# Expert weights, activations and hidden values as float16 pairs in place of float32r pairs, with scales measured on the chip

## The chip, the cores and the metric

One NeuronCore of a Trainium2 chip runs the whole program. The metric is the device time of one execution in microseconds (us), as a median over runs. TensorE is the matmul engine, VectorE (DVE in the profile), ScalarE (ACT) and GpSimd (POOL) do the elementwise work, SyncE (SP) issues the DMAs. Matmul results land in PSUM, eight banks of 128 x 512 float32; everything else lives in SBUF.

## The reference

```python
# attention: q, k, v are (2, 8, 1152, 64); q is averaged over pairs of rows
q_pool = q.reshape(B, H, S // 2, 2, D).mean(axis=3)
scores = np.matmul(q_pool, k.transpose(0, 1, 3, 2)) / np.sqrt(D)
attn = softmax(scores)                       # with 1e-9 added to the sum
x = matmul(attn, v)  -> (1152, 512)
# experts: E = 4, w1 (4, 512, 1024), w2 (4, 1024, 512)
p = domain_probs / (domain_probs.sum(-1, keepdims=True) + 1e-09)
for e in range(E):
    h = np.maximum(x @ w1[e], 0.0)
    out += p[:, e:e + 1] * (h @ w2[e])
# last layers: w1, w2 (512, 1024), w3 (1024, 1024), w_out (1024, 512)
a = x @ w1;  b = x @ w2
return ((a * b) @ w3) @ w_out
```

All inputs are float32 but those of the last layers, which the kernel reads as 64-bit words and converts on the chip.

## The kernel before

The program has three stages, one after the other on TensorE.

The **attention** runs over eight pairs of heads. An agenda holds closures with times in units of one block of scores (`at(t, f)`); sorted by time, it gives the program order, which each engine then follows. Per pair, `plan_v` measures the range of v: VectorE takes the maximum of each partition (line 409), TensorE transposes the two columns of maxima (413), VectorE reduces them to one number per head and makes a power of two of it in a chain of small operations (418 to 424), a tiny matmul with `ones2` spreads it to all partitions (427), and VectorE copies it (431). v is then held as a float16 high part (ScalarE, 441) and low part (VectorE, 445). The attention's output comes out multiplied back to its own scale into `X`.

The **experts** are cut into 16 groups `g` of 256 hidden columns, `PER` = 4 groups to an expert. Every product is taken from high and low parts, in three passes (`PASSES`: high x high, high x low, low x high). The parts are float32r, a 32-bit form in which the matmul reads float32 data:

```python
nc.scalar.copy(out=dst[:, 0, :], in_=src)
(eng or nc.gpsimd).tensor_tensor(out=dst[:, 1, :], in0=src, in1=f32(dst[:, 0, :]), op=ALU.subtract)
```

`prep_w(g, m)` loads w1 (m = 0) or w2 (m = 1) of a group (512 KB, line 567) into one of two `raw` buffers and splits it: ScalarE the high part (559), GpSimd the low part (560), VectorE for the first three. `rows_tile` transposes 128 rows of x and splits them into `xA` or `xB` (670, 674). `up_tiles` is the first layer: for each half group, a tile of 512 columns (part A, rows 0 to 511 of x) and two of 320 (part B), 12 matmuls each (596); ScalarE takes the result out through Relu as the high part of `h` (602), VectorE makes the low part (606). `down_tiles` is the second layer: nine tiles of 128 rows, 6 matmuls of 512 columns each (636); VectorE multiplies a tile by the token's share of the expert and adds it to `x2A` or `x2B` (648, 650).

`TASKS` sets the order: part A of group 0, part B of group 0, then whole groups 1 to 15. Group 0 begins inside the attention's agenda, at `UA`; in the loop, task n does the first layer of its group, then two calls of `prep_w`, then the second layer of task n - 1. Results rotate through eight banks (`bank`). The weights that are ahead of their use wait in four `spl` buffers.

Beside the loop, `tick` converts weights of the last layers from 64-bit words to float32: a load (700), one pass of ScalarE (705), five operations on VectorE (710 to 720, "a join"), one on GpSimd (723). There is one tick per task from n = 3 and two from n = 9.

The **last layers** multiply w3 by w_out first (1003), then do the gated product (1034) and the output (1051), all float32r, as before and after the change.

Of the kernel before, what the change touches and what calls it, by code (L numbers as in the profile page):

```python
# [47 lines left out]
SW = 130  # L48
W0 = 124
WD = 4  # L50
WS = 6
# [17 lines left out]
AX = mybir.AxisListType  # L69
PSUM = bass.MemoryType.PSUM  # L70


# [7 lines left out]
def tile_kernel(ctx: ExitStack, tc: tile.TileContext, q, k, v, dp, w1, w2, mw1, mw2, mw3, mwo, out):  # L80
# [18 lines left out]
    EPS = 1e-9  # L99

    f32 = lambda ap: ap.bitcast(F32)
    mm = nc.tensor.matmul
# [299 lines left out]
    def plan_v(i, t, te):  # L402


        st = {}

        def rows():
            m = st["m"] = tiny.tile([P, 2], F32, tag="vm", name=f"vm{i}")
            nc.vector.tensor_reduce(out=m, in_=rv[i], axis=AX.X, op=ALU.max, apply_absolute_value=True)  # L409

        def turn():
            st["p"] = work(1, f"vt{i}")
            nc.tensor.transpose(st["p"][0:2, 0, :P], st["m"], ident)
# [12 lines left out]
        def spread():  # L426
            mm(st["p"][:, 0, P : P + 2], ones2, st["d"], start=True, stop=True)

        def keep():
            vs[i] = tiny.tile([P, 2], F32, tag="vs", bufs=3, name=f"vs{i}")  # L430
            nc.vector.tensor_copy(vs[i], st["p"][:, 0, P : P + 2])
# [129 lines left out]

    def prep_w(g, m, eng=None):

        e, o = divmod(g, PER)
        t = raw.tile([P, 2 * DM], F32, tag="raw", name=f"rw{g}_{m}")
        src = (w1[e, :, o * GRP : (o + 1) * GRP], w2[e, o * GRP : (o + 1) * GRP, :])[m]
        nc.sync.dma_start(
            out=t.rearrange("p (c f) -> p c f", f=src.shape[1]), in_=src.rearrange("(c p) f -> p c f", p=P)
        )

        def rest():
            w = (w1s, w2s)[m][g] = spl.tile([P, 2, 2 * DM], F32R, tag="spl", name=f"w{m}_{g}")
            split(t, w, eng)

        return rest

    def up_tiles(n, space, h_tiles):
# [3 lines left out]
        for fc in range(2):  # L581
            for lo, hi in cuts(part):
# [18 lines left out]
                def to_hi(fc=fc, lo=lo, hi=hi, st=st):  # L601
                    nc.scalar.activation(out=hid[n][0][:, fc, lo:hi], in_=st["p"], func=AF.Relu)  # L602

                def to_lo(fc=fc, lo=lo, hi=hi, st=st):
                    hh, hl = hid[n]
                    nc.vector.scalar_tensor_tensor(  # L606
                        out=hl[:, fc, lo:hi], in0=st["p"], scalar=0.0, in1=f32(hh[:, fc, lo:hi]),
                        op0=ALU.max, op1=ALU.subtract,
                    )
# [13 lines left out]
    def down_tiles(n, space):  # L623
        part, g = TASKS[n]
        out_ = []
        for t in blocks(part):
# [14 lines left out]
            def add(t=t, st=st):  # L641
                x = "A" if t < NB else "B"
                if x not in x2:
                    x2[x] = xpool.tile([P, NB + 1, DM], F32, tag="x", name=f"x2{x}")
                acc, e = x2_of(t), g // PER
                share = pr[:, t, e : e + 1]
                if g == 0:
# [8 lines left out]

    def rows_tile(src, t, space, name):

# [4 lines left out]
        def pe():  # L663
            p = st["p"] = space(name)
            for d in range(KD):
                nc.tensor.transpose(p[:, d * P : (d + 1) * P], src(t)[:, d * P : (d + 1) * P], ident)

        def to_hi():
            p4 = st["p"].rearrange("p (d t) -> p d t", d=KD)
            nc.scalar.copy(out=xt[x][0][:, :, sl], in_=p4)  # L670

        def to_lo():
            p4 = st["p"].rearrange("p (d t) -> p d t", d=KD)
            nc.vector.tensor_tensor(  # L674
                out=xt[x][1][:, :, sl], in0=p4, in1=f32(xt[x][0][:, :, sl]), op=ALU.subtract
            )

        return pe, to_hi, to_lo

    def new_xt(x, pool, name):  # L680
        n = NTA if x == "A" else NTB
        xt[x] = [pool.tile([P, KD, n], F32R, tag=f"x{x}{m}", name=f"{name}{x}{m}") for m in range(2)]

# [44 lines left out]
    with tc.manual_schedule():  # L728
# [86 lines left out]
        def h_small(n):  # L815
            return [ha_p.tile([P, 2, NTA], F32R, tag=f"ha{m}", name=f"ha{n}_{m}") for m in range(2)]

        def plan_w(g, m, t):
            st = {}

            def load():
                st["rest"] = prep_w(g, m, nc.vector)

            at(t, load)
            at(t + WS, lambda: st["rest"]())

        for n, (g, m) in enumerate(((0, 0), (0, 1), (1, 0))):
            plan_w(g, m, W0 + WD * n)
        at(SW, experts)
        at(SW, new_xt, "A", xa_p, "x")  # L830
        at(SW, lambda: nc.sync.dma_start(out=XT[0:64], in_=X[0][64:128, NB, :]))
        t = SW + XA
        for n in range(NB):
            pe, to_hi, to_lo = rows_tile(x_src, n, one_bank, f"xt{n}")
            at(t + XS * n, pe)
# [4 lines left out]
        def rows_b():  # L840
            kstack.close()
            xb_p.append(ctx.enter_context(tc.tile_pool(name="xb_p", bufs=1, side="left")))
            new_xt("B", xb_p[0], "x")

# [15 lines left out]
        for _, _, f, args in sorted(agenda, key=lambda x: x[:2]):  # L860
# [4 lines left out]
        (r4, h4, l4), (r5, h5, l5), (r6, h6, l6), (r7, h7, l7), (r8, h8, l8) = (  # L865
            rows_tile(x_src, t, s_bank if t < 6 else one_bank, f"xt{t}") for t in range(NB, 9)
        )
# [17 lines left out]
    def h_large(n):  # L885
        return [h_p.tile([P, 2, NT], F32R, tag="h", name=f"h{n}_{m}") for m in range(2)]

    wo_s = [wo_p.tile([P, 2, 2, DM], F32R, name=f"wo{n}") for n in range(4)]

    with tc.manual_schedule():  # L890
# [52 lines left out]

        last_task = len(TASKS) - 1
        for n in range(1, last_task + 1):
            ups = up_tiles(n, bank, h_large)
            for num, steps in enumerate(ups):
                run(steps)
                if num == 2 and n >= 3:
                    tick(NF + 12)  # L950
            g = TASKS[n][1]
            if g + 2 < NG:
                prep_w(g + 2, 0)()
            if g + 1 < NG:
                prep_w(g + 1, 1)()
            if n > 1:
                for num, steps in enumerate(down_tiles(n - 1, bank)):
                    run(steps)
                    if num == 4 and n >= 9:
                        tick(NF + 12)  # L960
# [135 lines left out]
```

## Time and profile before

| | |
|---|---|
| median of 3 runs | 884.58 us (884.54 to 886.27) |
| profiled execution, its own time | 885.5 us |
| its span, first to last instruction | 883.7 us |
| mean granted TensorE clock | 0.992 |
| TensorE matmuls busy | 851.2 us, 96% |
| VectorE, ScalarE, GpSimd busy | 557.1, 358.7, 378.9 us |
| second layer of the experts, matmuls | 840 of 395 ns, 24 of 412 ns |
| first layer, 512 and 320 columns | 384 of 391 ns, 768 of 309 ns |

Matmuls overlap in the engine, so the length of one is more than the distance to the next: the busy time of a line says little, the distance between starts says what a matmul costs. Idle time of an engine matters only where another waits for it; the chain of waits tells that, followed back from the last instruction. PEclk in the windows is the granted share of TensorE's full clock.

### The profile page before, as it was taken

To read this page: it belongs to the slowest core of one execution; us is meant where nothing else is said; L and a number is where in the kernel's file an instruction comes from. 1 tells how busy PE (TensorE), PEld (TensorE's weight loads), DVE (VectorE), ACT (ScalarE), POOL (GpSimd) and SP (SyncE) were. 2 spreads that over 40 slices of the span, in tenths; PEclk is the share of its full clock that TensorE was granted. 3 is DMA by queue.
4 is the path that set the end of the run, shared out by engine and by line. 5 is a ranking of instruction groups with operands and counts; after the bars stand their busy time and mean duration, and the time that the engine had idled before them with its cause. 6 is when DMAs were issued, how large, how long until landed. Compare 5 with 4: busy or idle time off the path is not lost.

```text
span 883.7 us, 15735 instructions
## 1 busy us (share of the span) xinstructions
PE 851.2 (96%) x6356; PEld 737.9 (83%) x6356; DVE 557.1 (63%) x892; ACT 358.7 (41%) x632; POOL 378.9 (43%) x297
## 2 busy tenths in 40 slices
PE   7699999999999999999999999999999999998998
PEld 5588888888878888888888888888888889988887
DVE  6888988898785343455456665656567874996000
ACT  2577878787873312222222232222204333333211
POOL 4487888778751312223223343232210244666200
PEclk9799999999999999999999999999999999999999
DMA  8565756683540220211223223212210320330011
GB/s 189 152 145 147 174 140 149 142 175 91 128 121 3 96 71 24 72 39 36 70 72 96 77 90 96 96 46 75 72 48 1 95 93 28 96 96 24 12 48 47
DMA packets 59831, 76.72 MB, mean 87 GB/s; under 512 B 23480, under 2 KB 41264, under 8 KB 59760
## 3 DMA queue, kind: packets, MB, share of 16 engines
q1 hardware_dynamic: 59760, 75.73, 31.8%
q8 instruction: 50, 0.82, 0.4%
q14 instruction: 21, 0.17, 0.1%
HBM read 51.92 MB, written 2.36 MB: 61 GB/s over the span
## 4 chain that ended last, share of the span: by engine, by line
PE 70%; DVE 21%; issue 4%; DMA 2%; ACT 1%; SPq 1%; POOL 0%; DVEq 0%; ACTq 0%; POOLq 0%
PE up L596 23%; PE dn L636 22%; DVE mx L340 6%; PE o L1051 6%; PE wf L1003 5%; PE gt L1034 5%; PE s L465 3%; DVE vt L445 3%; PE mp L337 2%; DVE cv_a L716 2%; PE av L511 1%; DVE cv_a L710 1%; DVE cv_a L713 1%; DVE vm L409 1%; DVE pl L486 1%
## 5 line engine op out<-in xcount | busy, mean ns | idle before, releaser
L636 PE MATMUL dn<-w,h 128*128 128x512 f32 x840 | 199.6, 395 | 0.0
L636 PEld LDWEIGHTS dn<-w,h 128*128 128x128 f32 x840 | 156.5, 187 | 36.6
L486 POOL TENSOR_TENSOR pl<-p,ph 128x576 f16<-128x576 f32 x124 | 167.0, 1361 | 42.5 <-ACT ph L481 34.3
L560 POOL TENSOR_TENSOR w<-rw,w 128x1024 fp32r<-128x1024 f32 x29 | 69.6, 2401 | 196.0 <-ACT w L559 184.7
L606 DVE SCALAR_TENSOR_TENSOR h<-up,h 128x320 fp32r<-128x320 f32 (+1 forms) x94 | 51.6, 554 | 106.7 <-ACT h L602 106.7
L596 PE MATMUL up<-xB,w 128*128 128x320 f32 x768 | 118.3, 309 | 0.0
L596 PEld LDWEIGHTS up<-xB,w 128*128 128x128 f32 x768 | 115.0, 188 | 2.8 <-issue 0.3
L340 DVE TENSOR_REDUCE mx<-mp 128x1 f32<-128x768 f32 (+1 forms) x144 | 101.8, 750 | 21.6 <-PE mp L337 21.3
L465 PE MATMUL s<-Q,K 128*128 128x288 f32 x576 | 111.8, 318 | 0.6 <-DMA Q<-ml 0.5
L474 ACT ACTIVATE p<-s 128x576 f32<-128x576 f32 x144 | 93.5, 649 | 35.9 <-PE s L465 28.4
L602 ACT ACTIVATE h<-up 128x320 fp32r<-128x320 f32 (+1 forms) x94 | 46.0, 489 | 131.8 <-PE up L596 131.0
L596 PE MATMUL up<-xA,w 128*128 128x512 f32 x384 | 94.1, 391 | 0.4 <-DVE xA L674 0.4
L559 ACT CAST w<-rw 128x1024 fp32r<-128x1024 f32 x32 | 33.4, 1047 | 141.9 <-PE dn L636 83.8
L465 PEld LDWEIGHTS s<-Q,K 128*128 128x128 f32 x576 | 84.8, 194 | 1.4 <-issue 0.6
L511 PE MATMUL av<-vt,ph 128*128 128x65 f16 x720 | 82.3, 193 | 1.0 <-DVE XT L526 0.9
L596 PEld LDWEIGHTS up<-xA,w 128*128 128x128 f32 x384 | 71.0, 188 | 14.5 <-DVE xA L674 0.7
L511 PE MATMUL av<-vt,pl 128*128 128x65 f16 x720 | 82.4, 195 | 0.6 <-DVE pl L486 0.6
L481 ACT ACTIVATE ph<-s 128x576 f16<-128x576 f32 x128 | 82.7, 646 | 0.0
L509 PE MATMUL av<-vt,ph 128*128 128x64 f16 x720 | 81.6, 193 | 0.0
L511 PEld LDWEIGHTS <-ph 128*128 128x128 f16 x720 | 66.8, 99 | 7.6 <-DVE XT L526 2.2
L650 DVE SCALAR_TENSOR_TENSOR x2B<-dn,pr,x2B 128x512 f32<-128x512 f32 x75 | 54.6, 749 | 26.0 <-PE dn L636 25.6
L509 PEld LDWEIGHTS <-ph 128*128 128x128 f16 x720 | 66.7, 97 | 5.1 <-issue 2.3
(137 smaller groups left out, 1282.7 us busy)
## 6 DMA issues: line engine op xcount, KB each, us to landing
rw<-in_moe_w SPq DMA_DIRECT2D x64, 512.0 KB
K<-kab SPq DMA_DIRECT2D x32, 288.0 KB
rk<-in_k SPq DMA_DIRECT2D x16, 288.0 KB
rv<-in_v SPq DMA_DIRECT2D x8, 576.0 KB
Q<-qh SPq DMA_DIRECT2D x32, 144.0 KB
K<-kl SPq DMA_DIRECT2D x16, 288.0 KB
rq<-in_q SPq DMA_DIRECT2D x8, 512.0 KB
rw<-in_moe_w_out SPq DMA_DIRECT2D x8, 512.0 KB
```

The costliest lines, as they stand in the source:

```text
L340: nc.vector.tensor_reduce(out=mx[i, s][:, j, g : g + 1], in_=st.pop((j, g))[:, :, :PC], axis=AX.XY, op=ALU.max)
L465: mm(ps[:, n, :HALF], a[s][:, cs], b[s][:, n * HALF : (n + 1) * HALF], start=first, stop=not first,)
L474: nc.scalar.activation(out=two(p32), in_=st["s"][:, :, :HALF], func=AF.Exp, scale=SCORE)
L481: nc.scalar.activation(out=two(o), in_=st["s"][:, :, :HALF], func=AF.Exp, scale=SCORE)
L486: eng.tensor_tensor(out=plt[i, s][:, c, :], in0=st["p"], in1=pht[i, s][:, c, :], op=ALU.subtract)
L509: mm(t[:, j, 0:D], p, vt[s][:, c, 0:D], start=False, stop=False)
L511: mm(t[:, j, :], p, vt[s][:, c, D:], start=(c == 0 and n == 0), stop=(c == NC - 1 and n == 2))
L560: (eng or nc.gpsimd).tensor_tensor(out=dst[:, 1, :], in0=src, in1=f32(dst[:, 0, :]), op=ALU.subtract)
L596: mm(p, w[:, a, c, fc * P : (fc + 1) * P], x[b][:, c, lo - o : hi - o], start=(c == 0 and a == b), stop=(c == KD - 1 and a == 1),)
L636: mm(p, hid[n][a][:, fc, t * P : (t + 1) * P], w[:, b, fc, :], start=(fc == 0 and a == b), stop=(fc == 1 and a == 1),)
L650: nc.vector.scalar_tensor_tensor(out=acc, in0=st["p"], scalar=share, in1=acc, op0=ALU.mult, op1=ALU.add)
L1051: mm(p, gt[c][:, a, t * P : (t + 1) * P], wf[c][:, b, lo:hi], start=(m == 0), stop=(m == 23))
```

## The change

Both layers' operands (weights, x, h) become float16 pairs. float16 has a short range, so each operand is scaled by a power of two taken from a range measured on the chip, and the scales are taken out again in the share by which a tile is added.

- The range of x is bounded by that of v: per batch, the smallest of the v scales (`cxp`, `cx`), one small operation per pair and, after the last pair of a batch, `at_rows`, four small operations that also fold the reciprocal and `HDOWN` into the shares `prx`.
- The range of a group's weights is measured as that of v is: `prep_w` now returns six steps for both weights of a group: `load` (two DMAs), `rows` (two maxima on VectorE), `turn` (a transpose on TensorE and a chain of six small operations on VectorE), `spread` (a tiny matmul with `ones2`, a copy, and the group's shares), and `cut(0)`, `cut(1)` (ScalarE the high part, VectorE the low part). GpSimd has no splits of expert weights any more. One `spl` buffer now holds both weights of a group.
- Group 0's steps stand in the agenda from `W0`, group 1's from `W1`, at the offsets `WT`. In the loop, `weights(n)` runs after each tile and takes the next step when `WN` tiles have gone by since the last one and the group is near enough (three tasks ahead for the first four steps, two for the cuts).
- `to_hi` of the first layer becomes two passes of ScalarE: Relu with 1 / `HDOWN` in place in PSUM, then a copy to float16.

```diff
+    def at_rows(b):
+        nc.vector.tensor_reduce(out=cx[:, b : b + 1], in_=cxp[:, b], axis=AX.X, op=ALU.min)
+        nc.vector.reciprocal(out=cxi[:, b : b + 1], in_=cx[:, b : b + 1])
+        for r, ts in ((slice(0, P), slice(NB * b, NB * b + NB)), (slice(64 * b, 64 * b + 64), slice(8, 9))):
+            nc.vector.tensor_scalar(
+                out=prx[r, ts], in0=pr[r, ts], scalar1=cxi[r, b : b + 1], scalar2=HDOWN, op0=ALU.mult, op1=ALU.mult
+            )
...
+    def prep_w(g, space, eng=None):
...
+        def rows():
+            st["m"] = wtiny.tile([P, 2], F32, tag="wm", name=f"wm{g}")
+            for m in range(2):
+                nc.vector.tensor_reduce(
+                    out=st["m"][:, m : m + 1], in_=raws[m], axis=AX.X, op=ALU.max, apply_absolute_value=True
+                )
+
+        def turn():
+            p = space(f"wr{g}")
+            nc.tensor.transpose(p[0:2, :P], st["m"], ident)
...
+            nc.vector.tensor_reduce(out=a[:, 0:1], in_=p[0:2, :P], axis=AX.X, op=ALU.max)
...
+        def spread():
+            p = space(f"ws{g}")
+            mm(p[:, :4], ones2, st["d"], start=True, stop=True)
+            wab[g] = wtiny.tile([P, 4], F32, tag="wab", name=f"wab{g}")
+            nc.vector.tensor_copy(wab[g], p[:, :4])
...
+        def cut(m):
+            if m == 0:
+                w = spl.tile([P, 2, 2, 2 * DM], F16, tag="spl", name=f"w{g}")
+                w1s[g], w2s[g] = w[:, 0], w[:, 1]
...
+            nc.scalar.activation(out=w[:, 0], in_=raws[m], func=AF.Copy, scale=c)
+            (eng or nc.vector).scalar_tensor_tensor(
+                out=w[:, 1], in0=raws[m], scalar=c, in1=w[:, 0], op0=ALU.mult, op1=ALU.subtract
+            )
...
-                    nc.scalar.activation(out=hid[n][0][:, fc, lo:hi], in_=st["p"], func=AF.Relu)
+                    nc.scalar.activation(out=st["p"], in_=st["p"], func=AF.Relu, scale=1 / HDOWN)
+                    nc.scalar.copy(out=hid[n][0][:, fc, lo:hi], in_=st["p"])
...
-        return [h_p.tile([P, 2, NT], F32R, tag="h", name=f"h{n}_{m}") for m in range(2)]
+        return [h_p.tile([P, 2, NT], F16, tag="h", name=f"h{n}_{m}") for m in range(2)]
...
+        coming = [(1, 1, later[0])]
+        for g in range(2, NG):
+            coming += [(g if k < 4 else g + 1, w, f) for k, (f, w) in enumerate(zip(prep_w(g, bank), WN))]
+        wait = [0]
+
+        def weights(n):
+            wait[0] += 1
+            while coming and wait[0] >= coming[0][1] and coming[0][0] <= n + 2:
+                wait[0] = 0
+                coming.pop(0)[2]()
...
                 run(steps)
+                weights(n)
                 if num == 2 and n >= 3:
                     tick(NF + 12)
-            g = TASKS[n][1]
-            if g + 2 < NG:
-                prep_w(g + 2, 0)()
-            if g + 1 < NG:
-                prep_w(g + 1, 1)()
```

Line numbers in the orders below are those of each program itself. VectorE in the late loop, around the first layer of task 11 (h is a low part, cv_a to r a join). Before:

```order
L606 SCALAR_TENSOR_TENSOR h_1_7045<-up_0_0_7046,h_0_7044 128x512
L606 SCALAR_TENSOR_TENSOR h_1_7045<-up_0_512_7061,h_0_7044 128x320
L606 SCALAR_TENSOR_TENSOR h_1_7045<-up_0_832_7076,h_0_7044 128x320
L710 TENSOR_SCALAR cv_a<-cv_a 128x512
L713 TENSOR_SCALAR cv_a<-cv_a 128x512
L716 SCALAR_TENSOR_TENSOR cv_a<-rw_6902,cv_a 128x512
L719 TENSOR_SCALAR r_0_7093<-cv_a 128x512
L720 SCALAR_TENSOR_TENSOR r_0_7093<-rw_6902,r_0_7093 128x512
L606 SCALAR_TENSOR_TENSOR h_1_7045<-up_1_0_7104,h_0_7044 128x512
L606 SCALAR_TENSOR_TENSOR h_1_7045<-up_1_512_7119,h_0_7044 128x320
```

The same stretch now, from the maxima (wm) of group 12 to the start of its chain (wa):

```order
L611 TENSOR_REDUCE wm_7372<-rw_0_7326 128x1
L611 TENSOR_REDUCE wm_7372<-rw_1_7328 128x1
L689 TENSOR_TENSOR h_1_7355<-up_0_512_7375,h_0_7354 128x320
L689 TENSOR_TENSOR h_1_7355<-up_0_832_7391,h_0_7354 128x320
L812 TENSOR_SCALAR cv_a<-cv_a 128x512
L815 TENSOR_SCALAR cv_a<-cv_a 128x512
L818 SCALAR_TENSOR_TENSOR cv_a<-rw_7194,cv_a 128x512
L821 TENSOR_SCALAR r_0_7409<-cv_a 128x512
L822 SCALAR_TENSOR_TENSOR r_0_7409<-rw_7194,r_0_7409 128x512
L689 TENSOR_TENSOR h_1_7355<-up_1_0_7420,h_0_7354 128x512
L689 TENSOR_TENSOR h_1_7355<-up_1_0_7420,h_0_7354 128x512
L689 TENSOR_TENSOR h_1_7355<-up_1_512_7436,h_0_7354 128x320
L620 TENSOR_REDUCE wa_7454<-wr_7452 2x1
```

The two maxima stand ahead of the join, and the chain, which the tiny matmul needs, behind it.

TensorE in the same task, at the step from second-layer tile 0 to tile 1 (dn is the tile, h and w its operands). Before:

```order
L636 MATMUL dn_0_7159<-w_9_6756,h_1_6845 128x512
L636 MATMUL dn_0_7159<-w_9_6756,h_0_6844 128x512 x2
L636 MATMUL dn_0_7159<-w_9_6756,h_1_6845 128x512
L636 MATMUL dn_1_7167<-w_9_6756,h_0_6844 128x512 x2
L636 MATMUL dn_1_7167<-w_9_6756,h_1_6845 128x512
```

And now, with the tiny matmul (ws) of group 12:

```order
L718 MATMUL dn_0_7478<-w_6889,h_0_7130 128x512
L718 LDWEIGHTS h_1_7131
L718 MATMUL dn_0_7478<-w_6889,h_1_7131 128x512
L637 MATMUL ws_7486<-wd_7455,ones_74 128x4
L718 LDWEIGHTS h_0_7130
L718 MATMUL dn_1_7492<-w_6889,h_0_7130 128x512
```

The tiny matmul stands between the two tiles, and tile 1 cannot start before it.

## Rows read from the trace of the kernel before

**Rows 1.** The chain in order of time: start us, us, what.

```profile
319.68 12.60 PE dn L636 x54
332.28 12.49 PE up L596 x72
...
645.89 18.20 PE dn L636 x78
```

**Rows 2.** Windows: us; busy PE, PEld, DVE, ACT, POOL; PEclk; DMA.

```profile
332.28:357.37 25.09, 25.09 (x127) 21.66 (x127) 10.11 (x15) 5.49 (x9) 4.81 (x2) 1.00 0.06 22
507.92:533.01 25.09, 25.09 (x128) 21.65 (x127) 16.18 (x26) 7.23 (x12) 10.04 (x6) 1.00 0.27 90
```

**Rows 3.** Timeline of one period: start us, us, engine line op out<-in xcount.

```profile
532.86 2.88 PE L596 MATMUL up<-xA,w 128*128 128x512 f32 x12
...
535.58 3.68 PE L596 MATMUL up<-xB,w 128*128 128x320 f32 x24
...
540.17 0.42 DVE L710 TENSOR_SCALAR cv_a<-cv_a 128x512 f32<-128x512 f32 x1
...
542.28 0.69 DVE L720 SCALAR_TENSOR_TENSOR r<-rw,r 128x512 f32<-128x512 uint32 x1
```

**Rows 4.** Timeline of TensorE, float16 matmuls of the start and of the attention.

```profile
13.06 0.45 PE L752 MATMUL warm<-idle 128*128 128x128 f16 x5
...
14.39 1.68 PE L752 MATMUL warm<-idle 128*128 128x128 f16 x27
...
269.80 0.20 PE L511 MATMUL av<-vt,ph 128*128 128x65 f16 x1
...
270.49 0.19 PE L509 MATMUL av<-vt,ph 128*128 128x64 f16 x1
```

**Rows 5.** Timeline, the range of v in the last pair, 216 to 219 us.

```profile
216.48 0.27 PE L413 MATMUL vt<-ident,vm 128*2 128x128 f32 x1 [0.29 <-DVE vm L409]
...
216.59 0.19 PE L511 MATMUL av<-vt,ph 128*128 128x65 f16 x1
...
216.79 0.28 DVE L418 TENSOR_REDUCE va<-vt 2x1 f32<-2x128 f32 x1
...
217.10 0.14 DVE L419 TENSOR_SCALAR va<-va 2x1 int32<-2x1 int32 x1
...
217.64 0.22 DVE L424 TENSOR_SCALAR vd<-ident,va 2x2 fp32r<-2x2 f32 x1
...
217.92 0.27 PE L427 MATMUL vt<-vd,ones 2*128 2x2 f32 x1
...
218.12 0.20 PE L511 MATMUL av<-vt,pl 128*128 128x65 f16 x1
```

**Rows 6.** Lines 409, 445 (duration ns min/median/max); page groups 602, 606, 650.

```profile
L409 DVE TENSOR_REDUCE vm<-rv x8: 1341/1344/1354, 17.2 to 215.0; 128x2 f32<-128x1152 f32 x8
...
L445 DVE SCALAR_TENSOR_TENSOR vt<-rv,vs,vt x16: 814/1802/2252, 27.7 to 261.6; 128x576 f16<-128x576 f32 x16
...
L606 DVE SCALAR_TENSOR_TENSOR h<-up,h 128x320 fp32r<-128x320 f32 (+1 forms) x94 | 51.6, 554 | 106.7 <-ACT h L602 106.7
...
L602 ACT ACTIVATE h<-up 128x320 fp32r<-128x320 f32 (+1 forms) x94 | 46.0, 489 | 131.8 <-PE up L596 131.0
...
L650 DVE SCALAR_TENSOR_TENSOR x2B<-dn,pr,x2B 128x512 f32<-128x512 f32 x75 | 54.6, 749 | 26.0 <-PE dn L636 25.6
```

**Rows 7.** Timeline, load of expert weights, 393 to 401 us.

```profile
393.87 0.94 SPq L567 DMA_DIRECT2D rw<-in_moe_w  x2
...
399.28 1.05 ACT L559 CAST w<-rw 128x1024 fp32r<-128x1024 f32 x1 [3.84 <-DMA rw<-in_moe_w]
```

**Rows 8.** Waits of TensorE: us in total, times, longest.

```profile
PE mp L337 <- DVE vs L431: 1.7, 6, 0.3
```

**Rows 9.** Timeline of VectorE where the experts begin, 242 to 250 us.

```profile
242.98 1.22 DVE L560 TENSOR_TENSOR w<-rw,w 128x1024 fp32r<-128x1024 f32 x1 [1.20 <-ACT w L559]
...
248.62 1.27 DVE L674 TENSOR_TENSOR xA<-xt,xA 128x512 fp32r<-128x512 f32 x2
```

More of the change, by code (lines that the diff above doesn't have):

```diff
@@ L48 @@
 SW = 130
-W0 = 124
-WD = 4
+W0 = 123.5
+W1 = 134
+WT = ((0, 4.6, 6.9, 8.2, 8.4, 10), (0, 7.0, 10.0, 11.5, 13.0))
+WN = (1, 4, 4, 2, 1, 1)
 WS = 6
@@ L116, in tile_kernel @@
     XT = const.tile([P, DM], F32, name="XT")
+    ones2 = const.tile([2, P], F32R, name="ones2")
+    cxp = const.tile([P, B, 2], F32, name="cxp")
+    cx = const.tile([P, B], F32, name="cx")
+    cxi = const.tile([P, B], F32, name="cxi")
+    prx = const.tile([P, 9, E], F32, name="prx")
+    wtiny = ctx.enter_context(tc.tile_pool(name="wtiny", bufs=4, side="left"))
     xstack = ExitStack()
@@ L430, in keep @@
             vs[i] = tiny.tile([P, 2], F32, tag="vs", bufs=3, name=f"vs{i}")
-            nc.vector.tensor_copy(vs[i], st["p"][:, 0, P : P + 2])
+            p = st["p"][:, 0, P : P + 2]
+            nc.vector.tensor_copy(vs[i], p)
+            b, n = divmod(i, NPAIR // B)
+            if n == 0:
+                nc.vector.tensor_copy(cxp[:, b], p)
+            else:
+                nc.vector.tensor_tensor(out=cxp[:, b], in0=p, in1=cxp[:, b], op=ALU.min)
+            if n == NPAIR // B - 1:
+                at_rows(b)
         at(t, rows)
@@ L655, in down_tiles, with rows_tile @@
         return out_
-    def rows_tile(src, t, space, name):
+    def rows_tile(src, t, space, name, scaled=False):
         x, o = ("A", 0) if t < NB else ("B", NB)
@@ L666, in pe, with pieces, new_xt @@
                 nc.tensor.transpose(p[:, d * P : (d + 1) * P], src(t)[:, d * P : (d + 1) * P], ident)
+        def pieces():
+            for b in range(B):
+                if t < 2 * NB and b == t // NB:
+                    yield slice(0, P), sl, cx[:, b : b + 1]
+                if t == 2 * NB:
+                    n = sl.start + 64 * b
+                    yield slice(64 * b, 64 * b + 64), slice(n, n + 64), cx[:, b : b + 1]
         def to_hi():
             p4 = st["p"].rearrange("p (d t) -> p d t", d=KD)
-            nc.scalar.copy(out=xt[x][0][:, :, sl], in_=p4)
+            if not scaled:
+                nc.scalar.copy(out=xt[x][0][:, :, sl], in_=p4)
+                return
+            for a, to, c in pieces():
+                nc.scalar.activation(out=xt[x][0][:, :, to], in_=p4[:, :, a], func=AF.Copy, scale=c)
         def to_lo():
             p4 = st["p"].rearrange("p (d t) -> p d t", d=KD)
-            nc.vector.tensor_tensor(
-                out=xt[x][1][:, :, sl], in0=p4, in1=f32(xt[x][0][:, :, sl]), op=ALU.subtract
-            )
+            if not scaled:
+                nc.vector.tensor_tensor(
+                    out=xt[x][1][:, :, sl], in0=p4, in1=f32(xt[x][0][:, :, sl]), op=ALU.subtract
+                )
+                return
+            for a, to, c in pieces():
+                nc.vector.scalar_tensor_tensor(
+                    out=xt[x][1][:, :, to], in0=p4[:, :, a], scalar=c, in1=xt[x][0][:, :, to],
+                    op0=ALU.mult, op1=ALU.subtract,
+                )
         return pe, to_hi, to_lo
-    def new_xt(x, pool, name):
+    def new_xt(x, pool, name, kind=F32R):
         n = NTA if x == "A" else NTB
-        xt[x] = [pool.tile([P, KD, n], F32R, tag=f"x{x}{m}", name=f"{name}{x}{m}") for m in range(2)]
+        xt[x] = [pool.tile([P, KD, n], kind, tag=f"x{x}{m}", name=f"{name}{x}{m}") for m in range(2)]
     def x_src(t):
@@ L815, in h_small, with plan_w @@
         def h_small(n):
[L816 to L828, printed above, removed]
+            return [ha_p.tile([P, 2, NTA], F16, tag=f"ha{m}", name=f"ha{n}_{m}") for m in range(2)]
+        later = []
+        def plan_w(g, t, space):
+            steps = prep_w(g, space, nc.vector)
+            for f, d in zip(steps, WT[g]):
+                at(t + d, f)
+            if g == 1:
+                later.append(steps[5])
+        plan_w(0, W0, one_bank)
+        plan_w(1, W1, one_bank)
         at(SW, experts)
-        at(SW, new_xt, "A", xa_p, "x")
+        at(SW, new_xt, "A", xa_p, "x", F16)
         at(SW, lambda: nc.sync.dma_start(out=XT[0:64], in_=X[0][64:128, NB, :]))
@@ L865, in tile_kernel @@
         (r4, h4, l4), (r5, h5, l5), (r6, h6, l6), (r7, h7, l7), (r8, h8, l8) = (
-            rows_tile(x_src, t, s_bank if t < 6 else one_bank, f"xt{t}") for t in range(NB, 9)
+            rows_tile(x_src, t, s_bank if t < 6 else one_bank, f"xt{t}", True) for t in range(NB, 9)
         )
@@ L958, in tile_kernel @@
                     run(steps)
+                    weights(n)
                     if num == 4 and n >= 9:
```

58 lines of the change are left out of this document (40 added, 18 removed).

## The prediction, before the changed kernel was run

> **What bounds the kernel now.** I read the chain of waits in order of time first, then the windows and the timeline of the expert stage. Busy TensorE alone would not tell the limit; the chain does: to 664 us it is one unbroken series of expert matmuls, second-layer and first-layer pieces in turn, 27 of them from 320 us on, of which one pair and the last (two tasks' tiles on end) are shown: 12.60 and 12.49 us [rows 1]. A group of 256 expert columns thus costs 25.09 us, and nothing else is ever waited for. The windows, each one such period long, say how much room the other engines have in it: VectorE is busy 10.1 us early in the stage and 16.2 us where the conversions of the last layers ("joins") run beside it [rows 2]. So in this stage a cheaper matmul shortens the time one for one, until VectorE, or a wait for it, takes over.
>
> **The matmuls.** Their number stays. Starts are 12.60 / 54 = 233.3 ns apart in the second layer [rows 1]. In the first, a tile of 512 columns takes 535.58 - 532.86 = 2.72 us for 12 [rows 3], 226.7 ns each, and what is left of 12.49 us for the 48 of 320 columns, (12.49 - 24 x 0.2267) / 48 = 146.9 ns. [...] No float16 matmul of this size is in the trace. [...] I take 3 ns over the columns: 216.3 and 136.3. Saved: 864 x 17.0 = 14.7 us (second layer), 384 x 10.4 = 4.0 us and 768 x 10.6 = 8.1 us (first layer), together **-26.8 us**; the bounds, 4.4 and 2.6 ns, give -24.0 and -27.6.
>
> [...]
>
> **Added on TensorE.** Each of the 16 groups gets one transpose and one tiny matmul that measure its weights' range. The kernel already does this pair for v: after the transpose the next matmul starts 0.11 us later, after the tiny one 0.20 us later [rows 5]. 16 x 0.31 = **+5.0 us**. The bounds are 0 (hidden behind a long matmul) and 8, half as much again, since behind a 512-column matmul nothing like it is in the trace.
>
> **Added on VectorE in the stage.** Per group: two maxima over 128x1024, by the v maximum (1344 ns for 1152 elements [rows 6]) in proportion 1.2 us each, 2.4; the chain of small operations after the transpose, from 216.79 to 217.64 + 0.22 [rows 5] and one more of 0.22, 1.3; a copy and the new shares, 0.35 by the small ones in the same rows; two low parts of 128x1024. The low part of v is the same operation on 576 elements, 814 ns at its shortest and 2252 at its longest [rows 6]; 448 more elements at the maximum's rate of 1.17 ns make 1.34 at best, 2.7 for two. Together 6.7 us on top of 10.1 to 16.2: 16.8 to 22.9 us in a period of 25.09 - 1.68 + 0.31 = 23.7 us. It fits, in the last third barely. GpSimd loses 29 splits, which nobody waited for, so that gains nothing. ScalarE's second pass over each first-layer tile, 0.49 us [rows 6], six times a period, is covered: what it makes is read only a whole first layer later; without that cover it would cost its own length per tile. Loading a group's two weights together moves no more bytes; the queue issues them once both low parts of the group before are done.
>
> **New waits.** Before, TensorE never waited for a range. Now it stops, in program order, at the transpose until both maxima are done, and at the tiny matmul until the chain is; everything behind it on TensorE waits too. The built program puts four tiles between load and maxima, four to the transpose, two to the tiny matmul. Two tiles are 2.6 us of second layer, or 2.9 of both. In that time VectorE must take out the tile before (0.75 us [rows 6], or for a first-layer tile two passes of ScalarE and its own, 0.49 + 0.49 + 0.55) and run the chain, 1.3: 2.05 or 2.8 us. Any backlog is then a wait. A join is a backlog of 542.28 + 0.69 - 540.17 = 2.8 us [rows 3], and it stands between maxima and transpose in groups 5, 11, 12 and 15; I give these 1.5 us each. Five more have their maxima, or what follows them, among second-layer tiles (7, 8, 9, 10, 14), where four tiles are 5.2 us and the weights land 5.4 us after the issue [rows 7]: 0.4 us each. **+8 us**, between 0 and 2.1 us (the join less the slack left) in each of 15 groups, 32.
>
> **In the attention.** After each v scale VectorE does one small operation more (0.14 us [rows 5]), twice a set of four (0.7). Matmuls do wait for that scale, six times [rows 8]. 8 x 0.14 + 1.4 = 2.5 us; I put two thirds on the path, **+1.7**, bounds 0 and 2.5.
>
> **Where the experts begin.** Ahead of the last xA split (end 249.9 us) VectorE now does two maxima, a chain, a copy with shares and one low part where it did one split of 1.22: 2.4 + 1.3 + 0.35 + 1.34 - 1.22 = 4.2 us more, against 1.20 us of idle time there [rows 9]. TensorE's first expert tile needs that split. A third such split, which stood between the two hidden tiles of that layer, moves away, so it may come out less. **+3 us**, bounds 0 and 6.
>
> What follows the experts is not touched: 0. **Sum**: -26.8 + 5.0 + 8 + 1.7 + 3 = -9.1 us, from the profiled execution's 885.5 us 876.4. That execution is 0.9 above the median of the runs, 884.58, so for the median I expect **875.5 us**.
>
> **Rivals.**
> *Nothing waits.* Maxima and chains find room, the start is absorbed. For: VectorE had 9 to 15 us free per period [rows 2]. Against: two tiles are only just as long as the chain. 884.6 - 26.8 + 5.0 + 1.7 + 1 = 865.5 us.
> *TensorE waits for VectorE at every tiny matmul* (slower). VectorE comes to its last third with 22.9 us of work in 23.7, stays late, and each group pays the 2.1 us above: -26.8 + 9.7 + 32 = +15, 899.5 us. It decides from (26.8 - 9.7) / 15 = 1.1 us per group. For: low parts as long as the longest of v, 2252 against 814 ns [rows 6], would take the rest of the room. Against: only the last third is so full, and with eight banks of matmul results VectorE may be late without stopping TensorE elsewhere.
> [...]
> [...]
>
> **How the numbers follow.** Some waits, the forecast: 0.50. Nothing waits: 0.25. Every group waits: 0.21. No faster stream: 0.03. Float16 pays more: 0.01. About 0.2% (1.8 us) is what a measurement of this kernel can tell from no change. The forecast's own range, 865 to 888, comes of -26.8 by 2.5 either way, waits from 2 to 17 and the two starts from 1 to 7; of its half some 0.05 lie within 0.2% of 884.6 and 0.02 are slower. Of the rival with waits in every group, those of 1.0 to 1.2 us fall within 0.2%: 0.04. So faster 0.43 + 0.25 = 0.68, same 0.05 + 0.04 = 0.09, slower 0.23. The range for 8 in 10 leaves out the worse half of the slow rivals and a little below: 864 to 890.
>
> **What would show it.** Second-layer tiles of 1.30 us and first-layer ones of 2.60 and 1.64: the stream is as I say; at 1.40 it isn't. A period of 23.7 us in the early groups and more in the late ones, with TensorE's idle time released by VectorE at the two new matmuls: the waits; a chain that stays on TensorE: the first rival. VectorE busy some 22 us per period in the last third: its load is as reckoned. The last xA split some 3 us later than at 249.9 us: the start. I would be wrong with a wait that I did not name, as for the first use of a group's weights, or with low parts of over 2 us.

## The result: 876.8 us, 0.94% faster

The changed kernel takes **876.77 us** (median of 4 runs, 875.1 to 877.26) against 884.56 for the kernel before (4 runs, 883.93 to 886.27): a ratio of 0.9906, 95% interval 0.9887 to 0.9925. The profiled execution took 875.1 us, its span is 873.3 (before: 885.5 and 883.7).

The chain of waits in order of time (start us, us, what), beside [rows 1]:

```profile
336.04 11.70 PE up L678 x72
347.74 0.11 PE wr L617
347.85 2.59 PE dn L718 x12
350.44 0.20 PE ws L637
350.64 9.17 PE dn L718 x42
```

The first layer's 72 matmuls went from 12.49 to 11.70 us. The second layer's 54 take 2.59 + 9.17 = 11.76 instead of 12.60, and the two new matmuls of a group's range (wr, ws) now stand in the chain with 0.11 and 0.20 us.

The same in the timeline of TensorE, beside [rows 3]:

```profile
335.88 2.75 PE L678 MATMUL up<-xA,w 128*128 128x512 f16 x12
338.47 3.42 PE L678 MATMUL up<-xB,w 128*128 128x320 f16 x24
341.73 2.75 PE L678 MATMUL up<-xA,w 128*128 128x512 f16 x12
```

338.47 - 335.88 = 2.59 us for 12 of 512 columns, 216 ns each (before: 226.7); 341.73 - 338.47 = 3.26 for 24 of 320 columns, 136 ns (146.9).

Windows, one period each (us; busy PE, PEld, DVE, ACT, POOL; PEclk; DMA), beside [rows 2]:

```profile
335.88:359.64 23.76, 23.76 (x129) 12.51 (x128) 15.67 (x28) 8.49 (x15) 0.00 (x0) 1.00 0.31 89
407.31:432.28 24.97, 24.13 (x132) 12.56 (x129) 20.07 (x38) 8.62 (x16) 3.13 (x2) 1.00 0.18 63
503.59:529.88 26.29, 23.88 (x129) 12.44 (x128) 22.35 (x41) 9.56 (x17) 4.76 (x4) 1.00 0.42 121
601.62:624.98 23.36, 23.36 (x128) 12.32 (x126) 14.71 (x26) 6.98 (x14) 2.54 (x2) 1.00 0.15 46
```

Most periods are 23.8 us against 25.09. Two are much longer (the second and the third row, in which the ranges of groups 8 and 12 are measured: 24.97 and 26.29 us), and the one in which no range is measured (last row) takes 23.36. VectorE's busy time rose from 10.1 to 15.7 us early and from 16.2 to some 22 us late.

Where the trace after stands against the one before: the first expert matmul comes at 256.60 instead of 249.14 us (+7.5), the first layer of group 2 at 312.11 instead of 307.02 (+5.1), the last second-layer block at 636.68 instead of 645.73 (-9.0). So up to that block the expert stage gained 16.5 us, and 7.5 had been lost ahead of it. Before, and after, a tile of attention scores (s) and the first expert matmul:

```profile
226.51 0.77 PE L465 MATMUL s<-Q,K 128*128 128x288 f32 x4
...
249.14 0.40 PE L596 MATMUL up<-xA,w 128*128 128x512 f32 x1
```

```profile
231.04 0.77 PE L494 MATMUL s<-Q,K 128*128 128x288 f32 x4
...
256.60 0.39 PE L678 MATMUL up<-xA,w 128*128 128x512 f16 x1
```

More than half of that loss has its place in these rows, VectorE and GpSimd near the end of the attention:

```profile
218.80 4.48 POOL L515 TENSOR_TENSOR pl<-p,ph 128x576 f16<-128x576 f32 x3 [0.30 <-ACT ph L510]
...
220.67 0.17 DVE L462 RECIPROCAL cxi<-cx 128x1 f32<-128x1 f32 x1
220.87 2.44 DVE L464 TENSOR_SCALAR prx<-pr,cxi 128x16 f32<-128x16 f32 x2
...
256.15 1.40 DVE L775 SCALAR_TENSOR_TENSOR xA<-xt,cx,xA 128x512 f16<-128x512 f32 x2
```

The two operations on the shares (prx), of 16 and 4 elements a partition, hold VectorE for 2.44 us beside a series of GpSimd; the same happens at 100.07 us for the first batch. Against the trace before, the score tiles ahead of the first set start 0.9 us earlier and those behind it 1.2 later; at the second set it goes from 1.1 to 4.5 us later. The last xA split ends at 257.55 us (before: 249.89).

### The profile page after: what moved, and what is told of

Same layout as the page of the kernel before. It is cut to its first block, busy times and chain, and to the rows that moved or that the text cites. A ratio compares the mean times of both kernels' runs of the same rounds, so it can differ in the third digit from the quotient of the medians.

```text
span 873.3 us, 16029 instructions
## 1 busy us (share of the span) xinstructions
PE 833.9 (95%) x6388; PEld 597.2 (68%) x6388; DVE 643.4 (74%) x1098; ACT 406.3 (47%) x729; POOL 307.0 (35%) x268
## 4 chain that ended last, share of the span: by engine, by line
PE 64%; DVE 26%; DMA 4%; issue 3%; ACT 1%; SPq 1%; POOL 0%; DVEq 0%; ACTq 0%; POOLq 0%
PE up L678 19%; PE dn L718 18%; PE o L1163 6%; DVE mx L352 5%; PE wf L1115 5%; PE gt L1146 5%; PE s L494 4%; PE mp L349 3%; DVE cv_a L818 2%; DVE vt L474 2%; PE av L540 2%; DVE cv_a L812 2%; DVE cv_a L815 2%; DMA rw<-in_moe_w 1%; DVE w L653 1%
## 5 line engine op out<-in xcount | busy, mean ns | idle before, releaser
L718 PE MATMUL dn<-w,h 128*128 128x512 f16 x840 | 186.4, 379 | 0.0
L678 PEld LDWEIGHTS <-w 128*128 128x128 f16 x1152 | 111.7, 98 | 76.0 <-issue 1.6
L718 PEld LDWEIGHTS <-h 128*128 128x128 f16 x840 | 81.6, 98 | 93.2
L684 ACT ACTIVATE up<-up 128x320 f32<-128x320 f32 (+1 forms) x96 | 45.7, 476 | 171.8 <-PE up L678 171.8
L678 PE MATMUL up<-xB,w 128*128 128x320 f16 x768 | 110.5, 299 | 0.6 <-DVE xB L775 0.5
L689 DVE TENSOR_TENSOR h<-up,h 128x320 f16<-128x320 f32 (+1 forms) x94 | 50.8, 551 | 55.8 <-ACT h L685 55.5
L678 PE MATMUL up<-xA,w 128*128 128x512 f16 x384 | 89.1, 379 | 0.6 <-DVE xA L775 0.6
L825 POOL TENSOR_TENSOR cv_x<-cv_x,cv_a 128x512 f32<-128x512 f32 x24 | 30.8, 1284 | 154.3 <-DVE cv_x L822 154.3
L540 PEld LDWEIGHTS <-pl 128*128 128x128 f16 x720 | 67.0, 98 | 3.9 <-issue 1.1
L349 PE MATMUL mp<-kab,QZ 128*128 128x384 f32 x216 | 58.3, 377 | 7.4 <-DVE mx L352 4.0
```

Source lines behind the costliest of these rows:

```text
L349: mm(ps[:, n, :PC], QZ[:, o : o + P], KAB[i][:, sl], start=True, stop=True)
L540: mm(t[:, j, :], p, vt[s][:, c, D:], start=(c == 0 and n == 0), stop=(c == NC - 1 and n == 2))
L678: mm(p, w[:, a, c, fc * P : (fc + 1) * P], x[b][:, c, lo - o : hi - o], start=(c == 0 and a == b), stop=(c == KD - 1 and a == 1),)
L718: mm(p, hid[n][a][:, fc, t * P : (t + 1) * P], w[:, b, fc, :], start=(fc == 0 and a == b), stop=(fc == 1 and a == 1),)
L825: nc.gpsimd.tensor_tensor(out=x, in0=x, in1=a.bitcast(F32), op=ALU.add)
```

## The experiments

All times are medians against the kernel before, run on the same chip in turn with it; its own medians in these series lie between 884.42 and 884.96 us, so times of two series can be set beside each other to about half a us. A start time in a single trace is looser: the change and four of the runs below, which are alike up to the experts, reach one and the same early score tile at 58.6 to 60.5 us (59.32 in the change, 60.29 before). From that early tile on, distances are steadier: to the score tile shown above it is 166.2 us before and 171.7 in the change, to the first expert matmul 188.9 and 197.3.

Theory after the result: TensorE's gain in the stage is as predicted; what is given back is (a) the two sets on the shares, (b) the ranges' own 0.41 us a group, (c) waits, above all in groups 8 and 12, (d) VectorE's new work where the experts begin. The main rival: VectorE as a whole is the limit, so that whatever is removed at one place comes back at another.

### The shares on GpSimd

```diff
-            nc.vector.tensor_scalar(
+            nc.gpsimd.tensor_scalar(
                 out=prx[r, ts], in0=pr[r, ts], scalar1=cxi[r, b : b + 1], scalar2=HDOWN, op0=ALU.mult, op1=ALU.mult
```

> Two pairs of small TENSOR_SCALARs (prx, 128x16 and 64x4) that rescale the router shares hold VectorE for 2.43 us each in the profile of the change, in the middle of the attention's chain, and the score blocks behind them start 2.2 and 2.9 us later than before the change. Here GpSimd does these four operations; nothing else moves. Theory (they sit on the path): most of 2 x 2.4 us comes back, the first expert matmul starts near 252 to 254 us instead of 256.6, and the time is 872 to 874.5 us against 876.8 for the change. Rival (the slack ahead of the experts takes such slips up, or the slip is that of the other new small operations): 876 to 877.5 us.

871.77 us, ratio 0.9847 (0.9834 to 0.9861), 5.0 us below the change. The line of the operation (ns min/median/max):

```profile
L464 POOL TENSOR_SCALAR prx<-pr,cxi x4: 270/276/278, 100.9 to 221.0; 128x16 f32<-128x16 f32 x2, 64x4 f32<-64x4 f32 x2
```

The score tile that came 4.5 us late now comes 0.8 late (167.3 us behind the early tile, against 171.7), the first expert matmul at 253.54 instead of 256.60. The theory holds; a little more came back than its range of 872 to 874.5 us has.

### The same four operations in another order of elements, and alone

```diff
-                out=prx[r, ts], in0=pr[r, ts], scalar1=cxi[r, b : b + 1], scalar2=HDOWN, op0=ALU.mult, op1=ALU.mult
+                out=prx[r, ts].rearrange("p j e -> p e j"), in0=pr[r, ts].rearrange("p j e -> p e j"), scalar1=cxi[r, b : b + 1], scalar2=HDOWN, op0=ALU.mult, op1=ALU.mult
```

> The four small operations on the shares stay on VectorE and at their places, with the same elements, but walk them in steps of 4 elements instead of one after the other. [...]

875.22 us, ratio 0.9889 (0.9875 to 0.9902), which overlaps the change's and is 3.45 us above the first run's 871.77. Its line, beside the change's own:

```profile
L464 DVE TENSOR_SCALAR prx<-pr,cxi x4: 1206/1211/1305, 99.5 to 222.8; 128x16 f32<-128x16 f32 x2, 64x4 f32<-64x4 f32 x2
```

```profile
L464 DVE TENSOR_SCALAR prx<-pr,cxi x4: 1199/1210/1311, 100.1 to 222.1; 128x16 f32<-128x16 f32 x2, 64x4 f32<-64x4 f32 x2
```

The order of the elements is not the reason: 1211 ns in steps of four, 1210 one after the other. Whether the operation waits for GpSimd, or is that slow by itself, the next run tells: on top of the first run's edit the four stand once more in three periods of the loop, without a reader.

```diff
+                if n in (2, 3, 4) and num == 1:
+                    for b in range(B):
...
+                            nc.vector.tensor_scalar(
+                                out=prz[r, ts], in0=pr[r, ts], scalar1=cxi[r, b : b + 1], scalar2=HDOWN, op0=ALU.mult, op1=ALU.mult
+                            )
```

> The shares' operations on GpSimd, as in the first run, and the same four operations once more on VectorE, into a buffer that nobody reads, in three periods of the loop in which GpSimd stands idle. Theory (beside GpSimd each waits for the end of GpSimd's instruction): alone each takes 0.15 to 0.35 us. Rival (the operation as such takes 1.2 us on VectorE): 1.2 us each here too.

```profile
L1068 DVE TENSOR_SCALAR prz<-pr,cxi x12: 215/222/230, 294.7 to 337.5; 128x16 f32<-128x16 f32 x6, 64x4 f32<-64x4 f32 x6
```

222 ns alone, 1210 beside GpSimd: it waits. (The run's single execution took 870.49 us.) In the change's trace each of the four ends within 0.04 us of the end of a GpSimd instruction (101.27, 102.50, 222.07 and 223.31 us beside 101.24, 102.47, 222.05 and 223.28).

### One scale for all later groups

```diff
+        def same():
+            wab[g] = wab[1]
...
+        if g > 1:
+            return [load, lambda: None, lambda: None, same, lambda: cut(0), lambda: cut(1)]
```

> Leaves out the measuring of the ranges for groups 2 to 15: they are cut with the scales of group 1, so their two maxima, the transpose, the tiny matmul and the chain of small VectorE operations between them are gone; loads, cuts and products stay where they are. Theory: each group pays 0.41 us of TensorE for the two (a period of 23.77 against 23.36 us in the profile of the change), and some 4 us in all are waits at the tiny matmul; 14 x 0.41 + 4.3 = 10 us go, 866 to 868 us. Rival A (the waits are VectorE's queue as a whole and pass to other places, only TensorE's own part goes): 870 to 872 us. Rival B (VectorE's 4 us per group less lets still other waits go, or the loads come earlier): under 865 us.

865.25 us, ratio 0.9779 (0.9766 to 0.9793): less than a us below the theory's range and as little above rival B's. All 13 full periods are now alike; the first, and as long a stretch late in the loop, where the change has its longest:

```profile
312.30:335.65 23.35, 23.35 (x127) 12.32 (x126) 13.31 (x19) 7.81 (x14) 0.00 (x0) 1.00 0.28 91
501.00:524.35 23.35, 23.35 (x128) 12.31 (x126) 18.96 (x30) 9.59 (x17) 3.93 (x3) 1.00 0.51 150
```

So a group's range costs 23.77 - 23.35 = 0.42 us without a wait, 0.31 as two matmuls [rows 5] and 0.1 where the stream is broken, and all ranges of the loop together, waits included, 11.5 us by the medians and 9.3 by the two traces between 312 us and the last second-layer block.

### The maxima twice

```diff
-            for m in range(2):
+            for m in (0, 1, 0, 1) if g > 1 else (0, 1):
```

> The two maxima of groups 2 to 15 are taken twice, which adds 2.4 us of VectorE per group ahead of the transpose, 34 us in all. VectorE is busy 14.7 to 22.4 us of a period of 23.8. Theory (a period only pays where the join of a narrow load falls between the maxima and the transpose; elsewhere there is room): two to four groups wait 2.4 us longer, +5 to +10 us, 882 to 887 us. Rival A (room everywhere): under 879 us. Rival B (VectorE is already the bound in the second half): eight or more groups pay, over 896 us.

894.52 us, ratio 1.0113 (1.0098 to 1.0127): 17.7 us slower than the change, more than the theory and just short of rival B. Waits of TensorE (us in total, times, longest), here and then in the change:

```profile
PE ws L637 <- DVE wd L630: 9.0, 7, 2.4
PE wr L617 <- DVE wm L611: 6.8, 8, 2.4
```

```profile
PE ws L637 <- DVE wd L630: 4.0, 4, 2.4
```

Nine of 13 periods are now over 23.9 us, and three of them are 26.87 us or more. So most of these groups have less than 2.4 us of room in the change, and 2.4 us more on VectorE a group bring it near the slow rival. The longest period, 28.14 us, has a second price. Windows around its wait of 2.35 us at the transpose:

```profile
428.00:430.00 2.00, 1.54 (x8) 0.49 (x5) 1.90 (x3) 0.00 (x0) 0.00 (x0) 1.00 0.00 0
430.00:432.00 2.00, 0.11 (x1) 0.11 (x2) 2.00 (x3) 0.00 (x0) 0.00 (x0) 0.93 0.00 0
432.00:434.00 2.00, 2.00 (x6) 0.73 (x5) 2.00 (x4) 0.00 (x0) 0.00 (x0) 0.50 0.00 0
434.00:436.00 2.00, 2.00 (x8) 0.73 (x6) 1.86 (x8) 0.00 (x0) 0.00 (x0) 0.72 0.00 0
```

TensorE stood still for most of 430 to 432, and then the granted clock is 0.50 and 0.72 where it is busy again.

### The tiny matmul later, twice

```diff
-WN = (1, 4, 4, 2, 1, 1)
+WN = (1, 4, 4, 4, 1, 1)
```

> In the loop the tiny matmul of a group is issued two tiles later after the transpose (four tiles instead of two); transpose, maxima, loads and cuts stay at their tiles. Theory (the waits at the tiny matmul, 4.0 us in 4 in the profile of the change, come from a chain on VectorE that is late by 0.5 to 2.4 us; 2 tiles are 2.6 us): nearly all of it goes, 873 to 874 us against 876.8. Rival (VectorE's lateness is met at another place, the adds or the cuts, a little later): 876 to 877.5 us.

910.82 us, ratio 1.0287 (1.0271 to 1.0304), far from both. The edit did more than its expectation says: with 15 tiles to a group instead of 13 the steps no longer run ahead of a task, which has 15 tiles itself (6 of the first layer, 9 of the second). So the first cut of every group came to stand a single tile ahead of the one that reads it, and the second cut right behind that.

```profile
PE up L678 <- ACT w L652: 17.7, 14, 2.1
PE up L678 <- DVE w L653: 10.9, 14, 0.9
```

All 14 groups wait there for both halves of their first cut, and the mean granted clock of its five executions is 0.979 to 0.984, where the change's four have 0.986 to 0.992. The run tells nothing on the question; it shows what cuts cost that no longer run ahead. A second edit keeps 13:

```diff
-WN = (1, 4, 4, 2, 1, 1)
+WN = (1, 4, 4, 4, 0, 0)
```

> In the loop the tiny matmul comes four tiles after the transpose instead of two, and both cuts follow in its own tile, so that the second cut, and with it the next load, stays at its tile (in the run before, cuts and loads had moved too, and the second cut had come to stand in the tile that uses it). Theory (the waits at the tiny matmul, 4.0 us in all, are a late chain on VectorE and nothing else hangs on it): 3 to 4 us go, 873 to 874 us against 876.8 for the change. Rival A (the lateness passes to the cuts, which then crowd the adds and the high and low parts of the hidden tiles): 876 us or more. Rival B (groups 8 and 12 are late by their load, so that the same lateness is met two tiles on): 875 to 876.5 us.

875.2 us, ratio 0.9891 (0.9875 to 0.9906), against 0.9906 (0.9887 to 0.9925) of the change: overlapping, nothing gained that can be told apart. Group 12 still waits, now at the transpose:

```profile
517.66 0.27 PE L617 MATMUL wr<-ident,wm 128*2 128x128 f32 x1 [1.63 <-DVE wm L611]
```

That is rival B: group 12's maxima are late. Rival A has a part too: the two periods up to 339 us are 1.6 us longer together than in the change, with 0.5 and 0.7 us in which the first layer waits for the two halves of a cut. Why group 12's maxima are late, the change's own timeline shows:

```profile
492.34 12.86 SPq L802 DMA_DIRECT2D rw<-in_moe_w  x2
505.29 0.94 SPq L603 DMA_DIRECT2D rw<-in_moe_w  x2
...
499.92 2.08 DVE L653 SCALAR_TENSOR_TENSOR w<-rw,wab,w 128x1024 f16<-128x1024 f32 x1
...
511.12 2.54 DVE L611 TENSOR_REDUCE wm<-rw 128x1 f32<-128x1024 f32 x2 [2.82 <-DMA rw<-in_moe_w]
...
519.31 0.27 PE L637 MATMUL ws<-wd,ones 2*128 2x4 f32 x1 [2.41 <-DVE wd L630]
```

The last low part of group 11 frees the buffers at 502.0, but SP's queue issues group 12's load (L603) only at 505.3: ahead of it a load for the last layers (L802, the "narrow" load of the expectations) waits for its own buffer, until a join has read it. The low part itself took 2.08 us, where most take 1.28. VectorE then stands idle for 2.82 us for the data, and TensorE 2.41 us for VectorE.

### The joins at other places

```diff
-                if num == 2 and n >= 3:
+                if num == (5 if n == 7 else 2) and n >= 3:
...
-                    if num == 4 and n >= 9:
+                    if num == 5 and n >= 9:
```

> The shares' operations on GpSimd, as in the first run, and the narrow loads with their joins stand at other tiles: those among the second layer's tiles one tile later (from group 12's point of view behind its own load in SP's queue, where before they stood ahead of it and held it while they waited for a free buffer), and the one in the period of group 8 three tiles later, out from between its two cuts. Theory (groups 8 and 12 pay 1.2 and 2.5 us because a join or a blocked narrow load makes their maxima late): periods of 24.95 and 26.26 us come down to 23.8 to 24.2, 868 to 869.5 us against 871.8 for the first run. Rival (VectorE's load as a whole makes them late, so that another group pays): 871 to 872.5 us.

869.04 us, ratio 0.9823 (0.9809 to 0.9836), 2.7 below the first run; the intervals just touch. Group 12's load now goes first and at 495.94, 4.1 us ahead of the start of its period, where in the change it came 1.7 us behind:

```profile
495.94 3.03 SPq L603 DMA_DIRECT2D rw<-in_moe_w  x2
502.04 9.88 SPq L802 DMA_DIRECT2D rw<-in_moe_w  x2
```

Its period went from 26.26 to 24.19 us. Group 8's went from 24.95 to 25.56, so that half of the edit was wrong: three tiles later the join stands still nearer to the maxima. The two periods make 1.5 of the 2.7 us by the traces; 1.4 stand ahead of the early tile (58.6 us against 60.0), where the two programs are alike.

### The maxima of group 0 earlier, and all together

The first of these two loads group 0 earlier and takes its maxima four tiles earlier, on top of the shares on GpSimd; the second takes them one at a time in two earlier pairs, with the joins moved as in the last run.

```diff
-W0 = 123.5
-WT = ((0, 4.6, 6.9, 8.2, 8.4, 10), (0, 7.0, 10.0, 11.5, 13.0))
+W0 = 115
+WT = ((0, 9.1, 15.4, 16.7, 16.9, 18.5), (0, 7.0, 10.0, 11.5, 13.0))
```

> The shares' operations on GpSimd, as in the first run, and besides that group 0 is loaded some ten score tiles earlier and its two maxima are taken four tiles earlier, where VectorE stands idle for some 0.4 to 0.9 us at a time, instead of right ahead of the last maxima of the attention, which they hold up by 2.3 us. Theory (that is where most of the experts' later start comes from): the first expert matmul comes 1.5 to 2.5 us earlier than in the first run (253.5 us), 869.5 to 870.5 us against 871.8. Rival (VectorE is full from 230 us on, so they hold up other maxima by as much): 871.5 to 872.5 us.

871.2 us, ratio 0.9846 (0.9828 to 0.9863): not to be told from the first run, as its rival says. The first expert matmul comes at 252.40, 1.1 us earlier, but 0.8 of that stood at the early tile already; counted from there it gained 0.3 us (193.2 against 193.5). The two maxima, one behind the other, now hold up score tiles some four tiles earlier, which start 2.0 us later than before the change where the first run's were 1.6 late.

```diff
-        def rows():
+        def rows(ms=(0, 1)):
...
+W0 = 64
+WT = ((0, 24.1, 66.1, 67.4, 67.9, 69.5), (0, 7.0, 10.0, 11.5, 13.0))
...
-                at(t + d, f)
+                at(t + d, f, *([(0,)] if d == 24.1 else []))
+            if g == 0:
+                at(t + 42.1, steps[1], (1,))
```

> All that helped, together: the shares on GpSimd, the joins at the other tiles, and group 0 loaded some seventy score tiles earlier with its two maxima taken one at a time, each in one of VectorE's idle spells behind the shift's split, in two different pairs. Theory (each maximum costs under 0.3 us there, and 2.5 us at the end of the attention are gained): the first expert matmul at 250.5 to 251.5 us and 866 to 868 us. Rival (the attention gives it all back, since VectorE is its bound all along): 868.5 to 869.5 us, as the run with the joins moved.

867.64 us, ratio 0.9806 (0.9792 to 0.9821). One maximum at a time finds room, each behind the low part of the scores' shift (ml), where VectorE had waited 0.88 us for TensorE in the first run:

```profile
173.39 1.20 DVE L612 TENSOR_REDUCE wm<-rw 128x1 f32<-128x1024 f32 x1
...
202.80 1.20 DVE L612 TENSOR_REDUCE wm<-rw 128x1 f32<-128x1024 f32 x1
```

The first expert matmul comes at 250.73, within the expectation (191.4 us behind the early score tile, against 193.5 in the first run and 193.8 in the one with the joins moved); the score tiles behind both maxima are no later than in the first run. The size of the piece and its place were changed together, so which of the two helped is not shown.

### Group 8's join first, and the tiny matmul later from group 8 on

```diff
-                if num == (5 if n == 7 else 2) and n >= 3:
+                if num == (0 if n == 7 else 2) and n >= 3:
```

> The joined version with one more place changed: in the period of group 8 the join stands behind the first up tile, where VectorE is idle for some 2 us, instead of behind the last. Theory (group 8's maxima are late by the 3 us of that join and the adds queued behind it): its period comes from 25.56 to 23.8 to 24.3 us and the time to 866 to 866.5 us against 867.6. Rival (the join only passes its delay on through the cuts to the same maxima): 25 us and more for that period, 867 to 868 us.

865.51 us, ratio 0.9787 (0.9773 to 0.98), 2.1 below the run before, where the intervals overlap. Group 8's period is 24.06 us instead of 25.56: the theory. The median is half a us under its range; the period makes 1.5 of the 2.1 us, and by the traces 0.7 stand ahead of the early tile, where nothing was changed.

```diff
-            coming += [(g if k < 4 else g + 1, w, f) for k, (f, w) in enumerate(zip(prep_w(g, bank), WN))]
+            coming += [(g if k < 4 else g + 1, w, f) for k, (f, w) in enumerate(zip(prep_w(g, bank), WN if g < 8 else (1, 4, 4, 4, 0, 0)))]
```

> As the run before, and from group 8 on the tiny matmul comes four tiles after the transpose and both cuts in its tile. Theory (what is left of the waits at the tiny matmul, 0.9 us at most each, is covered by two tiles): 0.5 to 1.5 us less than the run before, 865 to 866 us. Rival (crowding the two cuts costs as much as it saves, as in the earlier run with this placing): within 0.5 us of the run before.

**864.95 us**, ratio 0.9778 (0.9765 to 0.9791): 0.6 below the run before, where the intervals overlap, and 11.8 below the change. The times do not tell the theory from its rival; by the traces the periods of groups 8 and 12 are 0.3 and 0.4 us shorter than in the run before, that of group 9 is 0.3 longer. Groups 8 and 12, whose periods were 24.97 and 26.29:

```profile
400.61:424.38 23.77, 23.77 (x131) 12.49 (x129) 20.35 (x38) 8.65 (x16) 2.54 (x2) 1.00 0.21 67
495.98:519.74 23.76, 23.76 (x129) 12.52 (x128) 21.74 (x40) 9.57 (x17) 4.18 (x4) 1.00 0.41 123
```

With all ranges measured it is as fast as the run that left most of them out (which kept the change's attention), and it is faster than both kernels. The rival, VectorE as the limit everywhere, is out: VectorE does as much as in the change, in other places, and between 312 and 640 us the trace shows no wait of TensorE for it.

## Why the prediction was right, point by point

| term, us | predicted | profiled executions |
| --- | --- | --- |
| float16 stream | -26.8 | -27.8 (16 x (23.35 - 25.09)) |
| ranges on TensorE | +5.0 | +6.7 (16 x 0.42) |
| waits in the loop | +8 | +4.3 (13 periods, 312.87, less 12 x 23.77 and 23.36) |
| attention | +1.7 | +4.5 (score tile at 231.04 for 226.51; 5.5 from the early tile on) |
| start of the experts | +3 | +2.9 (7.46 less 4.53) |
| sum | -9.1 | -9.4 (-8.4 with 5.5); spans -10.4, medians -7.8 |

The profiled execution of the change is the fastest of its four. The prediction's range for its own forecast, 865 to 888, is a little narrower than the ends that it names, which add up to 863 and 889; nothing hangs on that.

- *The matmuls*: right: 216.3 and 136.3 ns predicted, 215.8 and 135.8 measured. What the columns alone take, over which the 3 ns and the bounds of 4.4 and 2.6 are put, no run shows; the two measured sizes differ by 80.0 ns for 192 columns, 0.417 ns a column, and by an estimate from these two numbers 2.5 ns stand over the columns in both. 512 columns, each with its own weight load, came at 216 ns.
- *Added on TensorE*: mis-sized by a third. The two matmuls are 0.11 and 0.20 as read [rows 5]; the missing 0.1 is in the second layer, 11.76 us with them and 11.65 without.
- *Added on VectorE*: 16.8 to 22.9 us predicted, 15.7 to 22.4 found. The low parts take 1.28 us, as reckoned; four of the 32 take 1.76 to 2.08, each begun while GpSimd was at work. That it "fits, in the last third barely" is too kind: with the maxima doubled all five periods from that of group 8 to that of group 12 are over 25.4 us, and the first of the 13 is over 25.
- *New waits*: the size was half, the places were wrong. Of the four groups given 1.5 us for a join between maxima and transpose (5, 11, 12, 15) 5 and 11 did not wait, 15 waited 0.4 us, and 12 waited 2.4, for another reason: its load. That "the queue issues them once both low parts of the group before are done" left out what else stands in SP's queue: the step that failed here. Group 8, given 0.4, cost 1.2 (0.84 as a wait); its cause is a join, as moving that join shows (24.06 us).
- *In the attention*: the term that failed most. The "set of four" was priced by the smallest operations of VectorE, 0.7 us a set. Two of the four take 2.4 us together, because GpSimd is at work beside them, and they stand on the chain; the first run gives 5.0 us back. With them on GpSimd the attention costs 1.1 us from the early score tile on, so the rest of the term was no larger than predicted.
- *Where the experts begin*: right in size; with group 0's two maxima taken elsewhere (one at a time, in the run of 867.64 us) 2.1 us come back, so they are most of it.
- *The rivals*: nothing waits (865.5) was not so, but 864.95 is what the kernel takes once the waits and what the attention lost are gone. Every group waits (899.5): 894.5 came of 2.4 us more VectorE work a group.

Two errors of opposite sign, +2.8 in the attention (3.8 from the early tile on) and -3.7 in the waits, cancel; that the median came within 1.3 us of 875.5 is in good part luck.

## What to carry to other kernels

A small operation beside a busy neighbour may be priced by what the neighbour runs at that time and not by its own length (here 1210 ns on VectorE beside GpSimd's 1.28 us, 222 alone): look for the longest row of the same kind beside it, not the shortest. A load that is issued once its buffer is free is late by whatever waits ahead of it in the same queue (here 3.3 us, from 502.0 to 505.29); put the load that TensorE depends on ahead of one that may block. Work that must be added to a nearly full engine belongs where it waits for others, in pieces of about the length of that wait: here 1.2 us in spells of 0.9 cost next to nothing.

## What the runs showed of the hardware

A VectorE TENSOR_SCALAR on 16 or 4 elements a partition took 222 ns alone; beside GpSimd's instructions of 1.28 us it took 1210, and 1211 with its elements in steps of four; on GpSimd itself, 276. Two small matmuls between large ones cost 0.42 us together (periods of 23.77 and 23.35 us), 0.1 more than their own distances of 0.11 and 0.20. In the run with the maxima twice, TensorE's wait of 2.35 us, which ended at 431.89, was followed by a granted clock of 0.50 from 432 to 434 us and of 0.72 from 434 to 436, while the change's own wait of 2.41 us, which ended at 519.31, left the clock at 1.00 in each window of 2 us from 515 to 525: the length of the wait alone did not decide it.
